# A third unit's sums in an output bank pair, bf16 transposes, and smaller moves at the two ends of a fused convolution and SiLU kernel

## The chip, the cores and the metric

The kernel runs on one core of one Trainium2 chip. The metric is the device time of one execution in microseconds (us). The kernel before takes 690.77 us, the median of three executions (690.75 to 691.17). PE is the matrix engine, DVE is VectorE, ACT is ScalarE, POOL is GpSimd, SP is the engine whose queue issues most DMAs.

## The reference, cut to what matters

```python
# x: (8, 4096, 192), weight: (8, 7); moe_w_in: (192, 2048), moe_w_out: (2048, 192), moe_beta: (2048,)
w = softmax(weight, axis=-1)                         # one 7-tap filter for each of 8 heads of 24 channels
c = einsum('hk,bskhg->bshg', w, windows(pad(x, 6)))  # causal convolution over the sequence
h = c.reshape(32768, 192) @ moe_w_in
g = h * sigmoid(moe_beta * h)                        # = SiLU(beta h) / beta
out = g @ moe_w_out                                  # (32768, 192), float32
```

## The kernel before

The tokens are cut into 32 stages of 1024 (two groups of 512). A stage has 16 units. A unit is six matmuls of 512 columns into a pair of PSUM banks ("hidden"), one SiLU of ScalarE that empties the pair into `g`, and eight pairs of matmuls of 192 columns that add `g @ w_out` into output banks ("output"). The kernel uses eight PSUM banks: two pairs `ph` for hidden sums, and the pairs `pa` and `pb` for output sums. The convolution runs on VectorE with a share on PE, ahead of the matmuls that need it. A tap is the shifted input times one of the seven filter weights; PE's taps multiply by a diagonal matrix and read the input in a type called fp32r. To evacuate a bank is to copy it out of PSUM. A load lands when its data have arrived. The change touches only the first stage and the last. There the input arrives, is transposed by PE, and the second chunk of tokens ("chunk 1") is prepared while the first units run:

```python
    def second():                                  # transposes chunk 1
        xt = new_xt(1)
        for i in range(2):
            pt = (in_b, in_a)[i]()                 # first half in pair pb, second in pair pa, fp32
            for b in range(2):
                for c in range(NG):
                    for r in range(2):
                        ...
                        nc.tensor.matmul(pt[:, r, o : o + DG], x1b[...], ident_b[rows, rows], ...)
            t = HALO + i * 2 * BLK
            for r in range(2):
                nc.vector.tensor_copy(xt[...], pt[...])     # VectorE empties the half
        halo(1, xt0)
        nc.vector.tensor_copy(xt1[:, HALO - PAD :], xt[:, 0, HALO - PAD :])   # the fp32r copy of chunk 1

    CONV1 = {4: (0, 2), 5: (2, 4), 6: (4, K)}      # PE's conv taps of chunk 1, behind units 4, 5, 6; they read xt1
    # ... cut ...
    for s in range(N_ST):
        for u in range(NF):
            if s > 0 or u > 1:
                hidden(s, u)
            elif u == 0:
                ...                                # hidden sums of units 0 and 1 fill both ph pairs
                second()
            if s > 0:
                output(s, u, 8 if s < N_ST - 1 else 7, "ab")
            # ... cut ...
            if s == 0 and u in CONV1:
                conv1(u)
    while waiting or any(slots.values()):
        output(N_ST, 0, 1, "ab")                   # whatever output pairs are left
```

## Time and profile before

| | before |
|---|---|
| time, median of three | 690.77 us |
| span of the profiled execution | 689.31 us |
| first SiLU starts | 13.16 us |
| stage 1 starts (its first hidden matmul) | 30.02 us |
| PE's last matmul ends | 685.90 us |

From the page of the kernel before: part 2 (40 slices of the span, tenths busy) and part 4 (the chain of waits, shares of the span).

```profile
PE   8999999999999999999999999999999999999997
ACT  7988888888888888888888888888888888888883
...
PE 99%; ACT 1%; issue 0%; DVE 0%; ACTq 0%
```

PE is busy from end to end, so between stage 1 and the last stage only fewer or shorter matmuls could help. What can be won lies in the first slice and the last.

The timeline of PE in the kernel before. The columns are: start in us, length in us, engine, line, operation, output and inputs, shapes, count, and in brackets the idle time before it with its releaser.

```profile
5.11 0.53 PE L233 MATMUL pb<-ident_b,x0b 128*128 128x128 bf16 x3
...
13.11 0.34 PE L367 MATMUL pb<-ident_b,x1b 64*128 64x64 bf16 x12
13.28 0.34 PE L367 MATMUL pa<-ident_b,x1b 64*128 64x64 bf16 x12
14.32 0.82 PE L423 MATMUL ph<-ct,w_in_s 64*128 64x512 bf16 x6 [0.70 <-ACT g L431]
15.33 0.82 PE L423 MATMUL ph<-ct,w_in_s 64*128 64x512 bf16 x6 [0.18 <-ACT g L431]
16.35 0.82 PE L423 MATMUL ph<-ct,w_in_s 64*128 64x512 bf16 x6 [0.20 <-ACT g L431]
...
677.22 0.35 PE L456 MATMUL pa<-w_out_s,g 64*128 64x192 bf16 x4
678.03 0.34 PE L456 MATMUL pa<-w_out_s,g 64*128 64x192 bf16 x4 [0.46 <-ACT g L431]
```

The three bracketed lines near 15 us are units 2, 3 and 4. Each waits until a SiLU has emptied a `ph` pair. The last line is the end: PE has run out of output matmuls and waits for the very last SiLU.

The timeline of VectorE in the kernel before, over the same stretch of the start:

```profile
15.55 0.43 DVE L383 CAST xt<-xt 128x518 fp32r<-128x518 bf16 x1
15.90 0.48 DVE L338 TENSOR_SCALAR ct<-xt,cw 128x1024 bf16<-128x1024 bf16 x1
16.30 0.95 DVE L314 TENSOR_TENSOR w_out_s<-w_out_raw,beta_r 128x768 bf16<-128x768 f32 x1
```

The first is the fp32r copy of chunk 1, the second the first VectorE tap behind it, the third the second of four scalings of `w_out`.

### The profile page before, as it was taken

Reading aid. Unit: us, or ns where it says so; the run is one execution under the profiler, and the core shown is the slowest. Engines: PE = TensorE matmul, PEld = TensorE weight load, DVE = VectorE, ACT = ScalarE, POOL = GpSimd, SP = SyncE. Lnnn points to the kernel's source line nnn. Section 1 sums busy time; section 2 is a strip of 40 time slices with the busy share of each in tenths; the row PEclk is TensorE's granted clock in tenths of the full one; section 3 lists DMA queues with packets and bytes.
Section 4 is the critical chain, followed back from the end, with each engine's and each line's share of the span. In section 5 each row is a group of like instructions: output and inputs, shape, how many; then the busy total and the mean of one; then the engine's idle time right before and its main releaser. Section 6 shows DMA issues by size and latency. Waiting matters only on the chain.

```text
span 689.3 us, 24341 instructions
## 1 busy us (share of the span) xinstructions
PE 683.1 (99%) x11312; PEld 521.5 (76%) x11312; DVE 523.8 (76%) x467; ACT 579.2 (84%) x531; POOL 8.3 (1%) x19
## 2 busy tenths in 40 slices
PE   8999999999999999999999999999999999999997
PEld 4677777777777777777777777777777777777776
DVE  6889877788777797777797777887777977777712
ACT  7988888888888888888888888888888888888883
POOL 4000000000000000000000000000000000000000
PEclk9999999999999999999999999999999999999999
DMA  9744333244332344333353332444322443322111
GB/s 230 185 104 117 105 100 88 62 113 116 94 105 74 79 116 115 96 99 61 97 117 105 94 98 59 112 117 104 95 70 82 117 116 88 105 55 58 49 36 59
DMA packets 121862, 67.06 MB, mean 97 GB/s; under 512 B 53264, under 2 KB 121760, under 8 KB 121760
## 3 DMA queue, kind: packets, MB, share of 16 engines
q1 hardware_dynamic: 119760, 63.93, 34.4%
q0 software_dynamic: 1664, 1.38, 1.2%
q8 instruction: 88, 1.44, 0.9%
q10 hardware_dynamic: 336, 0.21, 0.1%
q14 instruction: 14, 0.11, 0.1%
HBM read 29.89 MB, written 25.17 MB: 80 GB/s over the span
## 4 chain that ended last, share of the span: by engine, by line
PE 99%; ACT 1%; issue 0%; DVE 0%; ACTq 0%
PE ph L423 48%; PE pa L456 25%; PE pb L456 24%; PE ph L223 1%; ACT g L431 1%; PE pb L289 0%; PE ph L289 0%; PE pb L233 0%; PE ph L233 0%; PE pa L244 0%; PE pa L289 0%; ACT osb L472 0%; PE pa L308 0%; DVE zeros L178 0%; DVE warm L180 0%
## 5 line engine op out<-in xcount | busy, mean ns | idle before, releaser
L431 ACT ACTIVATE g<-ph,beta 128x1024 bf16<-128x1024 f32 x512 | 569.6, 1114 | 95.7 <-PE ph L423 89.8
L456 PEld LDWEIGHTS <-g 64*128 64x128 bf16 x8160 | 370.5, 94 | 103.1 <-ACT g L431 0.7
L423 PE MATMUL ph<-ct,w_in_s 64*128 64x512 bf16 x3072 | 424.0, 376 | 1.1 <-ACT g L431 1.1
L340 DVE SCALAR_TENSOR_TENSOR ct<-xt,cw,ct 128x1536 bf16<-128x1536 bf16 (+2 forms) x190 | 337.0, 1774 | 2.5
L456 PE MATMUL pa<-w_out_s,g 64*128 64x192 bf16 x4112 | 245.3, 243 | 0.5 <-ACT g L431 0.5
L456 PE MATMUL pb<-w_out_s,g 64*128 64x192 bf16 (+1 forms) x4048 | 230.6, 243 | 0.0
L423 PEld LDWEIGHTS <-w_in_s 64*128 64x128 bf16 x3072 | 159.6, 94 | 55.2 <-issue 2.9
L474 DVE TENSOR_REDUCE osb<-pa 128x384 f32<-128x768 f32 x64 | 61.3, 958 | 124.3 <-PE pa L456 123.1
L474 DVE TENSOR_REDUCE osb<-pb 128x384 f32<-128x768 f32 x63 | 60.3, 958 | 27.9 <-PE pb L456 27.9
L106 DVE CAST xb<-xf 128x768 bf16<-128x768 f32 x60 | 40.5, 677 | 0.0
L338 DVE TENSOR_SCALAR ct<-xt,cw 128x1536 bf16<-128x1536 bf16 (+2 forms) x32 | 31.2, 974 | 0.8 <-ACT xt L304 0.8
L223 PE MATMUL ph<-zeros 128*128 128x512 bf16 (+2 forms) x11 | 5.1, 576 | 1.1 <-DVE warm L180 1.1
L472 ACT COPY osb<-pb 128x192 f32<-128x192 f32 x1 | 0.3, 319 | 6.6 <-PE pb L456 6.6
L211 POOL DMA_DIRECT2D w_in_s<-in_moe_w_in_dram x8 | 5.3, 669 | 0.0
L121 DVE COPY xt<-xt 128x18 bf16<-128x18 bf16 x27 | 4.5, 166 | 0.0
L289 PE MATMUL pb<-xt,diag 64*128 64x512 f32 (+1 forms) x21 | 4.4, 435 | 0.0
L289 PEld LDWEIGHTS pb<-xt,diag 64*128 64x128 f32 (+1 forms) x21 | 2.6, 187 | 0.6
L223 PEld LDWEIGHTS <-zeros 128*128 128x128 bf16 x11 | 1.3, 131 | 2.2 <-issue 1.1
L314 DVE TENSOR_TENSOR w_out_s<-w_out_raw,beta_r 128x768 bf16<-128x768 f32 x3 | 2.8, 950 | 0.0
L181 ACT ACT_TABLE_LOAD x1 | 1.3, 1283 | 1.8 <-issue 1.8
L233 PEld LDWEIGHTS <-x0b 128*128 128x128 bf16 x12 | 1.3, 135 | 1.0 <-issue 0.5
L226 ACT CAST x1b<-x 128x384 bf16<-128x384 f32 x3 | 2.0, 716 | 0.0
(54 smaller groups left out, 28.0 us busy)
## 6 DMA issues: line engine op xcount, KB each, us to landing
out_dram<-osb SPq DMA_DIRECT2D x127, 192.0 KB, 2.2
xf<-in_x_dram SPq DMA_DIRECT2D x60, 384.0 KB, 4.2
xt<-xb SPq DMA_TRANSPOSE x120, 2.5
x<-in_x_dram SPq DMA_DIRECT2D x4, 384.0 KB, 4.9
w_out_raw<-in_moe_w_out_dram SPq DMA_DIRECT2D x4, 384.0 KB, 13.0
w_in_s<-in_moe_w_in_dram POOLq DMA_DIRECT2D x6, 192.0 KB, 10.6
w_in_raw<-in_moe_w_in_dram SPq DMA_DIRECT2D x2, 192.0 KB, 6.0
w_in_s<-in_moe_w_in_dram POOLq DMA_DIRECT2D x2, 96.0 KB, 7.8
```

Source lines behind the costliest of these rows:

```text
L106: nc.vector.tensor_copy(xbs[ch][:, :, :, h, :], xfs[ch][:, h].rearrange("q b (p c) -> q b c p", c=NG),)
L121: nc.vector.tensor_copy(dst, last[:, :, HALO + TOK - PAD :])
L211: nc.gpsimd.dma_start(out=w_in_s[r * DG : (r + 1) * DG, :, c0:c1], in_=w_in_v[:, :, c0:c1])
L223: nc.tensor.matmul(pf[:, 0, 0:cols], zeros, zc, start=True, stop=True)
L289: nc.tensor.matmul(pv, diag[rows, k, :], xt[rows, o : o + TOK], start=(k == k0), stop=(k == K - 1),)
L314: (nc.vector if i else nc.gpsimd).tensor_tensor(w_out_s[:, fcs, :], w_out_raw[:, fcs, :], beta_r[:, fcs].unsqueeze(2).to_broadcast((128, N ...
L338: nc.vector.tensor_scalar_mul(dst, src, scalar)
L340: nc.vector.scalar_tensor_tensor(out=dst, in0=src, scalar=scalar, in1=dst, op0=ALU.mult, op1=ALU.add)
L423: nc.tensor.matmul(ph[:, h, :], w_in_s[rows, j, fc * 128 : (fc + 1) * 128], cts[s][rows, j, :], start=(j == 0), stop=(j == NG - 1),)
L431: nc.scalar.activation(gs[s][:, fc], ph, AF.Silu, scale=beta[:, fc : fc + 1])
L456: nc.tensor.matmul(self.po[:, r, b * D : (b + 1) * D], g[rows, fc, self.h, q * BLK : (q + 1) * BLK], w_out_s[rows, fc, :], start=(self.don ...
L474: nc.vector.tensor_reduce(dst, self.po[:, :, 0 : nb * D].rearrange("p r n -> p n r"), axis=mybir.AxisListType.X, op=ALU.add,)
```

## The change

Its intent is to take PE's waits out of the start and the end. Unit 2 gets the pair `pa`, so that it need not wait for a SiLU; for this both transposed halves of chunk 1 share the pair `pb`, in bf16. One PE conv tap of chunk 1 moves ahead of unit 4, into time in which PE was seen to wait. The second scaling of `w_out` moves from VectorE to POOL. Warm-up matmuls on zeros (`fill`) get shorter, one evacuation moves to VectorE, the later diagonals are built behind the transposes of chunk 0, the last stage does six output pairs a unit instead of seven, and the last two stores move from the ACT to the SP queue. The diff is cut; `conv1` also takes its range of taps as arguments now.

```diff
-    diags(2, 4)
-    diags(4, K)
@@ transposes of chunk 0
-        nc.scalar.copy(tokens(xt0, b), pt)
+        (nc.vector.tensor_copy if b == 2 else nc.scalar.copy)(tokens(xt0, b), pt)
         if b % 2:
-            fill(1, 384)
+            fill(1, 384 if b > 1 else 128)
+    diags(2, 4)
+    diags(4, K)
@@
-    fill(1, 256)
+    fill(1, 128)
@@ scale_w_out
-        (nc.vector if i else nc.gpsimd).tensor_tensor(
+        (nc.vector if i > 1 else nc.gpsimd).tensor_tensor(
@@
     scale_w_out(0)
+    scale_w_out(1)
@@ second()
+        pts = in_b()
         for i in range(2):
-            pt = (in_b, in_a)[i]()
+            pt = pts[:, :, i * TOK // 2 : (i + 1) * TOK // 2].bitcast(BF16)
...
-                        nc.tensor.matmul(
+                        nc.tensor.transpose(
...
+            if i == 0:
+                hidden(0, 2, ph=in_a())
@@
-    CONV1 = {4: (0, 2), 5: (2, 4), 6: (4, K)}
+    CONV1 = {4: (1, 3), 5: (3, 5), 6: (5, K)}
@@ the last two stores
-            (nc.scalar if nb == 1 else nc.sync).dma_start(
+            nc.sync.dma_start(
@@ first_work
-        4: [None, lambda: scale_w_out(1), None],
+        4: [None, None],
@@ main loop
+            if s == 0 and u == min(CONV1):
+                conv1(0, 1)
-            if s > 0 or u > 1:
+            if s > 0 or u > 2:
                 hidden(s, u)
@@
-                output(s, u, 8 if s < N_ST - 1 else 7, "ab")
+                output(s, u, 8 if s < N_ST - 1 else 6, "ab")
```

More of the change, by code (lines that the diff above doesn't have):

```diff
@@ L370, in second @@
                             ident_b[rows, rows],
-                            start=True,
-                            stop=True,
-                        )
+                        )
+            if i == 0:
+                hidden(0, 2, ph=in_a())
             t = HALO + i * 2 * BLK
@@ L383, in second, with conv1 @@
         nc.vector.tensor_copy(xt1[:, HALO - PAD :], xt[:, 0, HALO - PAD :])
-    CONV1 = {4: (0, 2), 5: (2, 4), 6: (4, K)}
+    CONV1 = {4: (1, 3), 5: (3, 5), 6: (5, K)}
     conv1_ps = []
-    def conv1(u):
+    def conv1(k0, k1):
         if not conv1_ps:
@@ L393, in conv1 @@
         pv = conv1_ps[0]
-        for k in range(*CONV1[u]):
+        for k in range(k0, k1):
             for r in range(2):
@@ L556 @@
                 if u in CONV1:
-                    conv1(u)
+                    conv1(*CONV1[u])
                 if u == min(CONV1):
```

## The prediction

> **What bounds it now.** The chain of waits gives PE 99% of the span, and the 40-slice row of PE is full except for the first and the last slice. In the middle one unit (six matmuls of 512 columns, then eight pairs of 192) starts every 1.307 us in the timeline, and ACT idles 0.19 us in each: PE-bound. The change leaves the number of these matmuls alone, so it can only win what PE loses at the two ends: about 20 us of start (timeline, 0 to 20 us) and the last 12 us. That is at most one or two us of 690.
>
> **Start, the first 13 us.** The shorter warm-up matmuls and the VectorE evacuation buy little. The third transpose group already waits for ScalarE's first evacuation (ends 6.17, PE at 6.23), the fourth for the second (6.58, PE at 6.63), and the last evacuation starts when PE delivers (7.14). The conv starts (7.93) after the last warm-up fill, which becomes 128 columns shorter: about 0.05 us. The diagonals end near 8.1 instead of 6.9 us; VectorE's taps then end near 11.7 instead of 11.3, still before PE's part at 11.87. First SiLU: 13.16 to about 13.1.
>
> **Start, 13 to 20 us.** Today PE waits 0.70, 0.18 and 0.20 us for SiLUs to free the hidden banks (units 2, 3, 4). With unit 2's sums in the freed output pair, they run at 13.2 instead of 14.32 and that work leaves the queue. Unit 4 then is limited by its weights (landing at 15.78) and by the early conv tap, which needs the fp32r copy of chunk 1 (ends 15.98 now, about 15.93 after): it starts at about 16.2 instead of 16.35. Each later unit with four tap matmuls costs 1.14 us (17.66 to 18.80); the last, with six, cost 1.35 and is cut to four. Unit 7: 20.15 to about 19.8. After that PE's own period (1.06) holds, so about 0.35 us stays won.
>
> **End.** In the last stage seven pairs a unit become six; the work is deferred, not removed. Behind the last hidden unit PE now has nine pairs, then idles 0.46 us for the last SiLU. With six pairs a unit I count 18 pairs there, at 0.082 us each 1.5 us: longer than the 1.38 us from the end of that hidden unit to its SiLU's end. The unit period becomes 1.14 us, ScalarE needs 1.11: no new wait. Gain about 0.45 us. The last stores from the SP instead of the ACT queue: neutral (both issue 0.03 us after the copy).
>
> **Risk.** The second w_out scaling moves from VectorE (0.95 us) to POOL, where it cannot begin before its load lands at 15.29; the first took 1.47 us there. That falls on VectorE's copy of chunk 1 (15.55 to 15.98; 0.43 us for 518 elements[...]). [...]No run here shows it yet. If so, the copy ends near 17.2, the early tap makes unit 4 wait for it, and the start loses about 0.95 us instead of gaining 0.35: total near 691.3. I give this 40%; without it 689.97.
>
> **Prediction.** 690.2 us, range 689.4 to 691.4. Faster by over 2%: 0.5%; within 2%: 99%; slower by over 2%: 0.5%.
>
> **Right if** PE's 0.46 us wait for ACT near 678 us vanishes; unit 2's hidden matmuls stand between the two halves' transposes; unit 8 starts near 20.8 us (22 if blocked); the middle keeps 1.307 us. **Wrong if** the fills' shortening leaves the PE clock low longer[...], or VectorE's copy stretches behind POOL.

Three passages are cut from it, but no term of its sum. Without a block the sum is 690.77 less 0.35 and 0.45, 689.97 us; with one, 690.77 plus 0.95 less 0.45, about 691.3. In the risk, "it" and "If so" stand for the copy of chunk 1 ending only after POOL's multiplication. That was my estimate then (15.29, 1.47 and 0.43 make 17.19 us); a_again below measured it, 1.72 us for the copy instead of 0.43. As to the clock, the trace's records of the kernel before have the rise at 7.25 us.

## The result, and the profile after

The changed kernel took 690.20, 691.84, 693.23 and 691.28 us in four executions, a median of 691.56, against 690.9 for the kernel before beside it. The ratio is 1.001, with a 95% interval from 0.9988 to 1.0033: the same at 2%. (A ratio is the mean time of one kernel's fast runs over that of the other's of the same rounds, so it is not quite the ratio of the medians quoted.) More telling than the median is the spread: 3 us, where the four executions of the kernel before lie within 0.42.

The profile fell on the fastest of the four. The timeline of PE in the changed kernel:

```profile
5.03 0.33 PE L233 MATMUL pb<-ident_b,x0b 128*128 128x128 bf16 x3
...
12.57 0.35 PE L369 MATMUL pb<-ident_b,x1b 64*128 64x64 bf16 x12
12.75 1.06 PE L425 MATMUL pa<-ct,w_in_s 64*128 64x512 bf16 x6
14.04 0.35 PE L369 MATMUL pb<-ident_b,x1b 64*128 64x64 bf16 x12 [0.24 <-DVE xt L378]
14.21 0.83 PE L425 MATMUL ph<-ct,w_in_s 64*128 64x512 bf16 x6
16.14 0.50 PE L287 MATMUL pb<-xt,diag 64*128 64x512 f32 x2 [1.10 <-DVE xt L385]
16.45 0.85 PE L425 MATMUL ph<-ct,w_in_s 64*128 64x512 bf16 x6
...
674.65 0.83 PE L425 MATMUL ph<-ct,w_in_s 64*128 64x512 bf16 x6
675.30 1.83 PE L458 MATMUL pa<-w_out_s,g 64*128 64x192 bf16 x40
676.95 2.82 PE L458 MATMUL pb<-w_out_s,g 64*128 64x192 bf16 x64
```

Unit 2 now starts at 12.75 us without a wait for a SiLU, as intended. (Its six matmuls take 1.06 us instead of 0.82: the second part of its weights landed only at 12.94 us.) But the second half's transposes wait 0.24 us for VectorE to empty the first half, and the early tap waits 1.10 us for the copy of chunk 1, with unit 4 (16.45) behind it. At the end no bracket is left: PE does not wait for the last SiLU any more.

The timelines of VectorE and then of POOL in the changed kernel:

```profile
12.97 1.02 DVE L378 COPY xt<-pb 128x384 bf16<-128x384 bf16 x2 [0.38 <-PE pb L369]
14.43 1.02 DVE L378 COPY xt<-pb 128x384 bf16<-128x384 bf16 x2 [0.44 <-PE pb L369]
15.57 0.43 DVE L385 CAST xt<-xt 128x518 fp32r<-128x518 bf16 x1
15.91 1.69 DVE L338 TENSOR_SCALAR ct<-xt,cw 128x1024 bf16<-128x1024 bf16 x1
```

```profile
15.83 1.49 POOL L314 TENSOR_TENSOR w_out_s<-w_out_raw,beta_r 128x768 bf16<-128x768 f32 x1 [1.69 <-DMA w_out_raw<-in_moe_w_out_dram]
```

The copy of chunk 1 (15.57) escaped POOL's scaling (15.83) by a quarter of a microsecond. The next VectorE operation did not: it takes 1.69 us instead of 0.48, and ends 0.28 us after POOL does.

Where the profiled span changed (689.31 to 688.50 us), from the starts and ends of instructions in the two traces (differences of the unrounded values):

| stretch | before | after | difference |
|---|---|---|---|
| start to first SiLU | 13.16 | 12.63 | -0.52 |
| first SiLU to stage 1 | 16.86 | 17.28 | +0.42 |
| stage 1 to PE's last matmul | 655.88 | 655.24 | -0.64 |
| PE's last matmul to the end | 3.41 | 3.34 | -0.07 |

The first line owes most to the clock and little to the change. Three transposes at 5 us last 0.53 us in the one profile and 0.33 us in the other, with the same shapes: PE's clock had already risen. The trace's clock records have the rise at 7.25 us before and at 4.97 us after. In four other profiles of changed kernels with the short fills the rise lay at 4.51, 5.45, 6.80 and 6.86 us, and the first conv tap followed it: 7.04, 7.50, 7.60 and 7.62 us (7.93 before, 7.27 after). In the two traces of the table the stretch at full clock is 682.666 us long, and its start lies elsewhere in each (7.25 and 4.97 us); what decides where, they do not show. So positions in the start are best compared from the first SiLU on. From there the new order of the start costs 0.42 us even in the good execution.

### The profile page after: what moved, and what is told of

It is laid out like the page before. It is cut to its first block, busy times and chain, and to the rows that moved or that the text cites. A ratio compares the mean times of both kernels' runs of the same rounds, so it can differ in the third digit from the quotient of the medians.

```text
span 688.5 us, 24344 instructions
## 1 busy us (share of the span) xinstructions
PE 682.2 (99%) x11312; PEld 521.3 (76%) x11312; DVE 524.7 (76%) x467; ACT 578.9 (84%) x530; POOL 9.7 (1%) x20
## 4 chain that ended last, share of the span: by engine, by line
PE 99%; DVE 0%; ACT 0%; issue 0%
PE ph L425 48%; PE pa L458 25%; PE pb L458 24%; PE pb L287 1%; PE ph L223 1%; DVE xt L378 0%; PE ph L287 0%; ACT xt L302 0%; PE pb L369 0%; PE pa L244 0%; PE pa L287 0%; DVE xt L385 0%; PE ph L233 0%; ACT osb L474 0%; PE pb L233 0%
## 5 line engine op out<-in xcount | busy, mean ns | idle before, releaser
L314 POOL TENSOR_TENSOR w_out_s<-w_out_raw,beta_r 128x768 bf16<-128x768 f32 x2 | 3.0, 1480 | 4.8 <-DVE beta_r L354 3.2
L378 DVE COPY xt<-pb 128x384 bf16<-128x384 bf16 x4 | 2.0, 552 | 0.8 <-PE pb L369 0.8
```

The lines of the kernel that those rows point to most:

```text
L314: (nc.vector if i > 1 else nc.gpsimd).tensor_tensor(w_out_s[:, fcs, :], w_out_raw[:, fcs, :], beta_r[:, fcs].unsqueeze(2).to_broadcast((12 ...
```

## The experiments

Each kernel ran five or six times, the kernels of one batch on one chip beside executions of the kernel before. "SC" below means that the second scaling of `w_out` is back on VectorE, in its old place. Two theories stood for the slow executions. C: the shortened warm-up fills let the clock rise late. P: POOL's scaling blocks VectorE's copy of chunk 1, depending on when the scaling's load lands.

| kernel | median us | range us | before beside it, median |
|---|---|---|---|
| a_again: changed kernel unaltered | 690.59 | 690.03 to 693.48 | 691.11 |
| a_scale_dve: SC | 690.46 | 690.03 to 691.00 | 691.11 |
| a_fills: old fills | 691.15 | 690.62 to 693.20 | 691.11 |
| a_fills_scale: old fills and SC | 690.62 | 690.40 to 690.71 | 691.11 |
| b_tail6: before, six pairs at the end | 690.33 | 690.22 to 690.56 | 691.56 |
| a_order: POOL's scaling behind the copy | 690.63 | 690.28 to 691.03 | 691.56 |
| a_force: SC, block forced | 693.33 | 691.65 to 693.64 | 691.56 |
| a_early: SC, transposes together | 690.16 | 690.02 to 690.22 | 691.56 |
| a_late_pool: taps at old places | 690.72 | 690.15 to 690.90 | 691.35 |
| a_late_dve: SC, taps at old places | 690.48 | 689.75 to 691.55 | 691.35 |
| a_early_late: SC, together, old places | 690.26 | 689.84 to 692.09 | 691.35 |
| a_force_late: SC, block forced, old places | 691.00 | 690.79 to 691.10 | 691.22 |

All of them gave correct results. Batches differ: the kernel before has medians from 691.11 to 691.56 us, so times are best compared within a batch (rows with the same number in the last column).

### The changed kernel again: a_again

No edit.

> The changed kernel unaltered, to see how its executions spread (690.20, 691.84, 693.23, 691.28 so far; the kernel before 690.75 to 691.17). Theory C (clock): with 384 columns of warm-up fill less, [...]the conv then runs at half speed: slow executions cost up to 3 us, and in a profile that fell on one the conv taps start 0.43 us apart instead of 0.23. Theory P[...]: the second w_out scaling on POOL starts when its load lands, and in slow executions it blocks VectorE's copy of chunk 1 (0.43 us becomes 1.5 or more), so slow ones cost about 1 us, not 3. Both expect a median of 690.5 to 692 and a spread of at least 1 us.

Measured: 693.48, 690.03, 690.35, 690.59 and 691.70 us; ratio 0.9992 (0.9979 to 1.0006). This time the profile fell on the slowest execution. The timelines of VectorE and of POOL in it:

```profile
15.89 1.72 DVE L385 CAST xt<-xt 128x518 fp32r<-128x518 bf16 x1
17.54 0.47 DVE L338 TENSOR_SCALAR ct<-xt,cw 128x1024 bf16<-128x1024 bf16 x1
```

```profile
15.87 1.47 POOL L314 TENSOR_TENSOR w_out_s<-w_out_raw,beta_r 128x768 bf16<-128x768 f32 x1 [1.41 <-DMA w_out_raw<-in_moe_w_out_dram]
```

The same two operations as before, with POOL 0.03 us ahead of the copy. Now the copy takes 1.72 us instead of 0.43. The load that starts POOL landed at almost the same time in both profiles (15.76 and 15.80 us); it was the copy that came 0.33 us later, with the first SiLU (12.63 and 12.96 us), which moves with the clock's rise (13.16 us with a rise at 7.25 us before, 12.63 with one at 4.97 after). So both sides of the race move. PE's waits between 13 and 20 us (total, times, longest), and then the busy time by stretch (start:end, length, busy time of PE with its matmuls, PE's clock as a fraction, DMA share, GB/s):

```profile
PE pb L287 <- DVE xt L385: 2.4, 1, 2.4
PE pb L369 <- DVE xt L378: 0.4, 1, 0.4
```

```profile
12.28:15.69 3.41, 2.67 (x42) 1.00 1.18 233
15.69:19.11 3.42, 1.35 (x14) 1.00 1.18 234
19.11:22.52 3.41, 3.41 (x18) 0.50 1.13 288
```

The third stretch is the one in which this trace's clock is at half, 0.50 from 19.11 to 22.52 us; the two before it are cut to the same length. PE waits 2.4 us for the copy and is busy for only 1.35 of the 3.42 us before the clock falls. Against the good profile, unit 4 starts 1.29 us later after the first SiLU (5.11 against 3.82), and from there to the start of unit 8 it takes 1.61 us more (6.18 against 4.56); together 2.91 of the 3.25 us by which the spans differ. The first SiLU's own 0.33 us is nearly all the rest.

### One part undone at a time: a_scale_dve, a_fills, a_fills_scale

```diff
 a_scale_dve
-        (nc.vector if i > 1 else nc.gpsimd).tensor_tensor(
+        (nc.vector if i else nc.gpsimd).tensor_tensor(
-    scale_w_out(1)
-        4: [None, None],
+        4: [None, lambda: scale_w_out(1), None],
 a_fills
-            fill(1, 384 if b > 1 else 128)
+            fill(1, 384)
-    fill(1, 128)
+    fill(1, 256)
 a_fills_scale: both
```

> Changed kernel with the second w_out scaling back on VectorE. Theory P: the spread shrinks to that of the kernel before (0.4 us) and the time is about 689.9 us. Theory C: the spread stays (over 1 us), the fast executions are near 690.2.

> Changed kernel with both warm-up fills at their old length (384 and 256 columns), the scaling still on POOL. Theory C: the spread shrinks to about 0.4 us, near 690.2 us or a little below. Theory P: the spread stays, up to 1 us above 690.2.

> Both undone: old fills and the scaling on VectorE. Both theories: a narrow spread (0.4 us) near 689.9 us, faster than the kernel before by about 0.8 to 1.0 us. If it spreads still, the cause lies in neither.

With the scaling off POOL none of these ten executions exceeds 691.0; of the 14 so far with it on POOL (the changed kernel and a_fills) seven exceed 691.2. With the old fills alone one still took 693.20 us, at a mean clock of 0.998 where the other four have 0.999 or 1.0. So theory C falls as the cause of the slow executions and P stands. The fills themselves are worth nothing that these runs can separate (690.46 against 690.62 us). The profile of a_fills, an execution of 691.15 us, shows a second, smaller source of spread. The timeline of PE in it:

```profile
13.61 0.39 PE L425 MATMUL pa<-ct,w_in_s 64*128 64x512 bf16 x1 [0.28 <-DMA w_in_s<-in_moe_w_in_dram]
14.32 0.82 PE L425 MATMUL pa<-ct,w_in_s 64*128 64x512 bf16 x5 [0.32 <-DMA w_in_s<-in_moe_w_in_dram]
14.77 0.46 PE L369 MATMUL pb<-ident_b,x1b 64*128 64x64 bf16 x9
17.07 0.50 PE L287 MATMUL pb<-xt,diag 64*128 64x512 f32 x2 [1.10 <-DVE xt L385]
```

The copy of chunk 1 was not blocked, but it ended 3.89 us after the first SiLU instead of 3.36 in the first changed profile. Unit 2 waited for its own weights, which landed at 14.28 us (12.94 in the first changed profile), and the second half's transposes stand behind unit 2 in PE's order. So the copy, the early tap and unit 4 (17.37) came late too. Unit 4's own weights, at 17.26 us instead of 15.87, were late as well but did not come last. In the kernel before both halves' transposes stand ahead of unit 2.

### Order instead of place: a_order

```diff
-    scale_w_out(1)                    # ahead of second()
@@ second(), behind the copy of chunk 1
+        nc.gpsimd.tensor_copy(hold, xt1[0:1, HALO : HALO + 1].bitcast(FP32))
+        scale_w_out(1)
```

> Changed kernel, second scaling still on POOL, but ordered behind VectorE's copy of chunk 1 (a one-element POOL copy reads the copy's result first). Theory P: the copy can no longer be blocked, POOL now always blocks the first tap behind it (0.48 us becomes about 1.7), which has slack; no execution over 691.2, median 690.2 to 690.7. Rival C (slow executions come from the shortened fills alone, whatever POOL does): still executions near 692 to 693.

Measured 690.28 to 691.03 us: as expected, except that what POOL met was not the first tap but the ones behind it. The scaling stays on POOL and none of five executions is slow. The times alone say so: in the profiled execution the scaling's load landed at 17.40 us, after the copy's end at 16.73, and would not have met the copy without the edit either. The timelines of POOL and of VectorE in it:

```profile
17.46 2.30 POOL L314 TENSOR_TENSOR w_out_s<-w_out_raw,beta_r 128x768 bf16<-128x768 f32 x1 [0.31 <-DMA w_out_raw<-in_moe_w_out_dram]
```

```profile
17.16 3.69 DVE L340 SCALAR_TENSOR_TENSOR ct<-xt,cw,ct 128x1024 bf16<-128x1024 bf16 x2
```

Here POOL came second and had to wait: 2.30 us instead of 1.47, behind a VectorE tap with two inputs that ran its usual 1.28 us. The next tap then waited for POOL: it took 2.37 us, and the two together 3.69 instead of the 2.60 of the kernel before.

### The block forced: a_force, a_force_late

```diff
 a_force (with SC)
@@ second(), behind the third evacuation of chunk 1
+                if i == 1 and r == 0:
+                    nc.gpsimd.tensor_tensor(busy, w_out_raw[:, 0:NQ, :]..., xt[:, :, t : t + BLK]..., ALU.mult)   # 768 elements, unread
 a_force_late (also)
-    CONV1 = {4: (1, 3), 5: (3, 5), 6: (5, K)}
+    CONV1 = {4: (0, 2), 5: (2, 4), 6: (4, K)}
-            if s == 0 and u == min(CONV1):
-                conv1(0, 1)
```

> Both scalings after the first on VectorE, but a POOL multiplication of 768 elements with two inputs, whose result nobody reads, is started by the third VectorE evacuation of chunk 1, so that it always runs when the copy of chunk 1 is due. Theory P: the copy (or the small halo copy ahead of it) ends only after POOL's 1.48 us, unit 4 starts near 17.4 us instead of 16.4 in every execution, every execution is at least 0.9 us above the one without it (690.46), and where the clock drops because of PE's wait, up to 3 us. Rival: POOL and VectorE do not exclude each other, the result stays at 690.0 to 691.0.

> The forced block of the copy of chunk 1 once more (POOL multiplication nobody reads), but with the conv taps at their old places behind unit 4. Theory: the damage needs the early tap in front of unit 4. Unit 4 then starts when its weights land (16.2 to 16.7 us) although the copy ends near 17.7; PE's longest wait in 14 to 20 us is near 1 us; the clock does not fall; 690.5 to 691.6, at least 1.5 us below the median of the forced block with the early tap (693.33). Rival (a blocked copy costs the same wherever the tap stands): 692 to 693.6.

The timelines of POOL and then of VectorE in a_force:

```profile
15.60 1.64 POOL L385 TENSOR_TENSOR busy<-w_out_raw,xt 128x768 f32<-128x768 f32 x1 [1.13 <-DVE xt L378]
```

```profile
15.90 1.36 DVE L121 CAST xt<-xt 128x18 bf16<-128x18 f32 x1
17.30 0.43 DVE L394 CAST xt<-xt 128x518 fp32r<-128x518 bf16 x1
```

An 18-element copy that takes 0.16 us elsewhere takes 1.36, until POOL is done; the copy of chunk 1 comes after it. Unit 4 started at 18.18 us, later than the 17.4 expected, and every execution is slower than any of a_order's in the same batch, in two clusters: 691.65 and 691.68 us at a mean clock of 0.999 or 1.0, and 693.33, 693.56 and 693.64 us at 0.997 or 0.998. In the profile, which belongs to the second cluster, PE was busy 1.12 of the 3.42 us from 15.56 to 18.98 us, and the clock was at 0.50 for the next 3.41 us. So a block costs about 1.0 us against a_order's 690.63 of the same batch (1.2 against a_scale_dve's 690.46 of another), and about 1.8 more in the second cluster, whose one profile shows the half clock; why the first cluster escaped it was not shown.

With the tap behind unit 4 the same forced block costs much less, 690.79 to 691.10 us. The timeline of PE in a_force_late:

```profile
15.97 0.82 PE L434 MATMUL ph<-ct,w_in_s 64*128 64x512 bf16 x5 [0.30 <-DMA w_in_s<-in_moe_w_in_dram]
16.42 0.54 PE L467 MATMUL pa<-w_out_s,g 64*128 64x192 bf16 x4
17.78 0.73 PE L288 MATMUL pb<-xt,diag 64*128 64x512 f32 x4 [0.82 <-DVE xt L394]
```

Unit 4 and its output pairs fill the time, the wait for the copy is 0.82 us instead of 2.3, PE is busy 2.59 of the 3.41 us from 16.63 to 20.04 us, and the clock stays at 1.00. So the clock fell behind 1.35 (a_again) and 1.12 us (a_force) of busy PE in 3.42 us, and not behind 2.59 here or 2.48 in 3.41 us (the first changed profile, 15.21 to 18.62 us); what decides it these traces do not show. The damage needed both: POOL's block and a tap in front of unit 4.

### The end alone: b_tail6

```diff
 the kernel before
-                output(s, u, 8 if s < N_ST - 1 else 7, "ab")
+                output(s, u, 8 if s < N_ST - 1 else 6, "ab")
```

> The kernel before with nothing but six pairs a unit in the last stage instead of seven. The profiles so far put PE's end minus the start of stage 1 at 655.88 us before and 655.24 in every changed kernel, so this alone should give 0.63 us: a median near 690.4 where the kernel before has 691.1, and PE's gap before the last SiLU's sums gone. If the end gives only the 0.46 us that the prediction named, the difference is 0.45; if the profiles' 0.63 came from elsewhere, it is smaller still.

Measured 690.33 us, ratio 0.9984 (0.9972 to 0.9997). Against the 691.56 us of the kernel before in this batch that is 1.2 us less, not the 0.63 expected; the interval, 0.2 to 1.9 us, is too wide to size the gain, though all five executions lie below all nine of the kernel before. The traces size it. Stage 1 to PE's last matmul is 655.24 us against 655.88: 0.64 us, within 0.08 us the same as in every changed kernel. The timeline of PE:

```profile
674.67 0.83 PE L423 MATMUL ph<-ct,w_in_s 64*128 64x512 bf16 x6
675.31 1.83 PE L456 MATMUL pa<-w_out_s,g 64*128 64x192 bf16 x40
676.96 2.82 PE L456 MATMUL pb<-w_out_s,g 64*128 64x192 bf16 x64
```

Forty matmuls follow the last hidden unit without a gap. The bracket of before said 0.46 us because it counts from the modelled end of the last matmul. Counted by starts, the gap was larger: 40 matmuls here begin within 1.65 us (675.31 to 676.96), 0.17 us for four; before, a group of four began at 677.22 and the next matmul at 678.03, 0.81 us later; 0.81 less 0.17 is 0.64.

### Why the start gained nothing: a_early, a_late_dve, a_early_late, a_late_pool

```diff
 a_early (with SC; cut): all 24 transposes first, then unit 2, then the four evacuations
-            if i == 0:
-                hidden(0, 2, ph=in_a())
+        hidden(0, 2, ph=in_a())          # behind both halves' transposes
 a_late_dve (with SC), a_late_pool (scaling on POOL): the taps as in a_force_late, no forced block
 a_early_late (with SC): both
```

> Changed kernel, second scaling on VectorE, both halves' transposes issued together ahead of the third unit, so that the second half no longer waits for VectorE to empty the first (same banks). If that wait is what kept the copy of chunk 1 from ending earlier (VectorE idle 0.44 us between the halves), the copy ends about 0.27 us earlier after the first SiLU and so does unit 4: median about 690.2 against 690.46. If not, no change.

> Changed kernel with the scaling still on POOL, but the conv taps of chunk 1 back at their old places: none ahead of unit 4, so that unit 4 does not stand behind the copy of chunk 1 in PE's order. Theory P with the early tap as the link: a blocked copy now delays only taps that come after unit 4, PE's idle stretch is at most about 1 us instead of 2 to 3, the clock does not fall, and no execution exceeds 692. Rival (any block of VectorE by POOL costs the same, whatever PE's order): executions near 693 remain.

> Changed kernel with the scaling on VectorE and the taps at their old places. Stage 1 began 17.28 us after the first SiLU in three profiles of the changed kernel without a blocked copy, 16.86 in the kernel before, 16.91 with the transposes issued together. If the early tap is a cause of that loss, it is 17.1 or less here; if only the wait for the banks is, it stays at 17.2 to 17.3. Median 690.2 to 690.5.

> Scaling on VectorE, transposes issued together, taps at their old places. If the early tap is worth anything, this is slower than the same kernel with it (690.16 us; stage 1 at 16.91 us after the first SiLU) by 0.1 to 0.3; if it is worth nothing or costs, it is 690.1 or less and 16.6 to 16.9.

The timelines of VectorE and then of PE in a_early:

```profile
13.54 1.95 DVE L379 COPY xt<-pb 128x384 bf16<-128x384 bf16 x4 [0.56 <-PE pb L370]
```

```profile
12.97 0.53 PE L370 MATMUL pb<-ident_b,x1b 64*128 64x64 bf16 x24
13.32 0.93 PE L426 MATMUL pa<-ct,w_in_s 64*128 64x512 bf16 x6
...
16.18 0.49 PE L287 MATMUL pb<-xt,diag 64*128 64x512 f32 x2 [1.16 <-DVE xt L386]
16.50 0.84 PE L426 MATMUL ph<-ct,w_in_s 64*128 64x512 bf16 x6
```

VectorE's four evacuations run in one piece, and stage 1 comes 16.91 us after the first SiLU: 0.37 of the lost 0.42 us are back (a_scale_dve, which differs in nothing else, has 17.29). So the wait for the shared banks was needed for the loss. It was not enough: a_late_dve keeps that wait, moves only the taps back, and has stage 1 16.90 us after the first SiLU, so by its own expectation (17.1 or less) the early tap is a cause too. The loss was a late copy, handed on to unit 4 by the tap in front of it. That the second half's transposes wait until the first half is out of the shared pair is in the trace of the changed kernel (0.24 us of PE, and 0.44 us of VectorE behind it); what would happen without the wait no run here shows.

But a_early only gets back to the kernel before (16.86). The waits of PE in a_late_dve between 12.5 and 20 us show what else holds:

```profile
PE ph L424 <- DMA w_in_s<-in_moe_w_in_dram: 0.6, 1, 0.6
PE pb L368 <- DVE xt L377: 0.4, 1, 0.4
```

Without the early tap, unit 4 waits 0.6 us for its own weights. In the traces of these kernels they land as follows (the later of the two loads), and unit 4 and stage 1 start:

| kernel | weights of unit 4 land | unit 4 starts | stage 1 starts | stage 1 after landing |
|---|---|---|---|---|
| before | 15.78 | 16.35 | 30.02 | 14.24 |
| after | 15.87 | 16.45 | 29.91 | 14.04 |
| a_scale_dve | 16.24 | 16.28 | 29.74 | 13.50 |
| a_fills | 17.26 | 17.37 | 30.83 | 13.57 |
| a_fills_scale | 16.05 | 16.66 | 30.11 | 14.06 |
| a_order | 16.59 | 17.19 | 30.64 | 14.06 |
| b_tail6 | 16.09 | 16.26 | 29.93 | 13.84 |
| a_early | 16.26 | 16.50 | 29.94 | 13.68 |
| a_late_dve | 16.22 | 16.27 | 29.93 | 13.71 |
| a_late_pool | 16.71 | about 16.8 | 30.43 | 13.71 |
| a_early_late | 16.29 | about 16.3 | 30.02 | 13.72 |

(The three kernels with a blocked copy are left out. In the rows of a_late_dve, a_late_pool and a_early_late the start is that of the matmuls that follow the landing; one of the six can go before.)

Stage 1 starts 13.44 to 13.46 us after unit 4 in the six kernels with the early tap (after, a_scale_dve, a_fills, a_fills_scale, a_order, a_early), and 13.66 to 13.68 us after it in the other five. So the early tap is worth 0.2 us, but it binds unit 4 to the copy of chunk 1: unit 4 starts 0.45 to 0.46 us after the copy ends. In a_scale_dve the copy ended at 15.83 us, early enough for unit 4 to start right behind its weights, and stage 1 came 13.50 us after their landing; in the other kernels with the tap the copy was what held unit 4. The kernel before was at 14.24 us from the landing, and b_tail6, with the same start, at 13.84. So 0.3 to 0.7 us was to be had at the start, how much depending on the loads, which land anywhere from 15.8 to 17.3 us.

In a_early_late the first SiLU came early, at 12.52 us, and stage 1 still did not: with the taps behind, unit 4 waited for its weights. The times hardly tell the two places of the tap apart (690.16 and 690.26 us, in different batches): behind, PE waits for weights; before, for the copy.

a_late_pool had no execution over 690.90, as expected, but its profile has no blocked copy either (POOL began at 16.96 us, after the copy's end at 16.45), so a_force_late is the better witness.

## Why the prediction was wrong, point by point

- **The middle is PE-bound and untouched: right.** From stage 1 to the start of the last stage both profiles take the same 627.6 us.
- **Shorter fills and the VectorE evacuation bring about 0.05 us: not contradicted.** The first SiLU moves with the clock's rise, by more than any effect of these edits. Where the clock rose at nearly the same time, the first conv tap came 0.07 us earlier with the short fills (a_force 7.44 us, a_fills_scale 7.51), but not the first SiLU (12.91 and 12.83).
- **The start: wrong.** The step that failed is "Unit 4 then is limited by its weights (landing at 15.78) and by the early conv tap", with "it starts at about 16.2" and "about 0.35 us stays won". The tap waited for a copy that I had ending at 15.93 us with a first SiLU at 13.1, 2.83 us behind it; measured, it ended at 16.00 with the SiLU at 12.63, 3.36 behind it, because the second half's transposes wait for VectorE (a_early). I had unit 4 0.27 us behind the copy; it came 0.45 us behind. So unit 4 started 3.82 us after the first SiLU, against 3.19 in the kernel before, and the tap taken from behind it gave only 0.21 of that back. In place of a gain of 0.35 us, the start lost 0.42 us from the first SiLU on. Unit 8 started at 21.02 us instead of 20.8, although the first SiLU came early. The landing of the weights, which I took from one profile as 15.78, is 16.1 to 16.7 in most others; that would have taken part of the gain even with an early copy (the table above).
- **The end: right mechanism, mis-sized.** The term "Gain about 0.45 us" is 0.64 us, shown alone by b_tail6.
- **The risk: the block and its size were right, its form was wrong and the clock was missing.** The runs show the block in both orders: the copy took 1.72 us instead of 0.43 (a_again), and POOL's scaling 2.30 instead of 1.47 behind a VectorE tap (a_order). I took the block for a matter of all executions or none, at 691.3 us. It is a race between a copy and a load, and comes out differently from execution to execution. In "the start loses about 0.95 us instead of gaining 0.35" the two cases are 1.30 us apart. Between the blocked and the good profile, unit 4 starts 1.29 us later after the first SiLU, as foreseen; but the start as a whole takes 2.91 us longer, since 1.61 us goes to a stretch at half clock (19.11 to 22.52 us in a_again) that I had not thought of. Against the kernel before the blocked start lost 3.3 us.
- **The total.** Counted from the first SiLU, the start's loss and the end's gain leave about 0.2 us in a good execution; a_scale_dve, free of the race, has 690.46 us. With the race, the nine executions of the changed kernel have a median of 691.28 us and reach 693.48. The stated range was narrower than one kernel's own spread: the first four executions have a median of 691.56 us, outside it, and the next five one of 690.59, inside it. Which side a few executions fall on is luck, and so is the nearness of 691.28 to the 691.3 that I gave for the blocked case, since it is the middle of a mixture.

What stays open: the execution of 693.23 us in the first result has a mean clock of 1.0, unlike the profiled slow one (0.997), so the half-clock stretch is not shown for it. The three between 691.2 and 691.9 may be blocked copies without the clock's fall (691.65 us when forced) or late weights (691.15 us in a_fills); they were not profiled. There are slow executions that POOL's scaling cannot explain: 691.55 us in a_late_dve and 692.09 in a_early_late, which have it on VectorE, and 692.40 and 692.85 us in the kernel before.

The version to keep, by one batch of five executions each, is a_early (690.16 us, ratio 0.9981, 0.9969 to 0.9994), or, with one character changed, b_tail6 (690.33 us): nearly all that these versions gained is in the end.

## What to carry to other kernels

When work moves to POOL, ask which VectorE copies can run at that time (one took 1.72 us here instead of 0.43) and what decides the order; where it was a DMA's landing, as here, the cost was a lottery (690.03 to 693.48 us in a_again). A dependency that fixes the order (a_order) showed no slow execution in five, without moving the work back. Before reordering an engine to fill its waits, look for the next thing that would hold it: here the copy behind the shared banks, and in some executions the weights' landing, came after the waits that were taken away. Don't put a matmul that waits for a shaky producer in front of one that is ready, since the cost can exceed the wait: in the two profiles where PE waited 2.4 and 2.3 us for the copy (a_again, a_force), 3.41 us at half clock followed.
